# Unread matmuls of 512 columns on TensorE in the opening of an attention and expert kernel

## The chip, the cores and the metric

The kernel runs on one core of a Trainium2 chip. The metric is device time in microseconds (us), from launch to the end of the core's work. The core has TensorE (matrix products, PE in the rows; PEld is its weight load), VectorE (DVE), ScalarE (ACT), GpSimd (POOL) and SyncE (SP, which here only issues DMAs). Each engine works its own queue in order, and waits on semaphores for the others. [...]

## The reference

Attention over 4 batches, 8 heads, 768 positions, head size 64, with a linear distance bias and a window of 96 keys besides 8 global ones; then a gate that gives each of the 3072 tokens to one of 8 experts of 384 places; then the experts' two matrix products.

```python
scores = scale * np.matmul(q, k.transpose(0, 1, 3, 2))
is_global = pos[None, :] < int(n_global)
is_local = (rel >= 0) & (rel < int(n_local))
scores = scores + bias[None, :, :, :]
scores = np.where(is_global | is_local, scores, -1000000000.0)
a = np.exp(scores - np.max(scores, axis=-1, keepdims=True))
attn = np.matmul(a / np.sum(a, axis=-1, keepdims=True), v)
...
logits = x @ w_gate          # tokens are given out by falling logit, 384 to an expert
out[mask] = np.maximum(x[mask] @ w1[e], 0.0) @ w2[e]
```

## The kernel before

Attention runs in 8 **units**. Unit u holds four heads of one batch (two units to a batch), that is two pairs of heads, n = 2u ("a") and n = 2u + 1 ("b"). The keys are cut into 7 tiles of 120 keys with the 8 global keys in front of each; a tile is seen by a window of 216 queries. The tiles are in three groups: 0 and 1, 2 and 3, 4 to 6. The steps have short names, with the unit or pair that they work on:

- KT, QT: VectorE transposes keys or queries in blocks (line 278). KB (ScalarE, 286), KS (GpSimd, 292 and 293) put the keys in place for TensorE; QO (303) does so for the queries.
- S0, S1, S2: TensorE's scores of the three groups, in f32, four heads side by side in strips of 32 rows (line 335). An f32 matmul shows as two instructions in the trace. S0 has 32 instructions, S1 has 32, S2 has 48. They write the PSUM banks ps0 and ps1, of which there is one set; only S1 of unit 0 writes the four spare banks po0, po1, t0 and t1 (named psx).
- BI: VectorE adds the distance bias and takes the scores out of PSUM into P (line 353), two instructions to a pair. The next group's scores need the banks that BI has read. EX: ScalarE's exponential on P (360). M0, M1: GpSimd adds up what a sum over keys needs (369 to 376).
- AV0, AV1: TensorE's product with the values (393), two halves of the queries. OT: ScalarE copies it out (400). SU: TensorE's sums and gate products (410, 414), into t0 or t1. LT: VectorE takes these out. TK, TO: transposes of finished outputs for the token matrix (492 and 511), from unit 1 on.

The order on every engine is written by hand. Unit 0 and the first half of unit 1 stand one step after the other (lines 613 to 664 of before); after that a loop goes through the table ORDER once for every turn, and each entry has a stage: an entry with stage 3 works on the unit three turns back. So in one turn TensorE has S1 and S2 of one unit, AV and SU of the unit before, and S0 of the unit after. In turn 3 the entries that matter here are BI0b and BI0a of unit 1 (VectorE), then S1 of unit 1 (TensorE), then AV0b, SUa of unit 0, then S2 of unit 1. Turn 2 has S0 of unit 1 for TensorE, and for VectorE the transposes of unit 2.

The constant `ones_bf` (128 x 128, bf16) is filled by GpSimd at the start (line 71). The loads of keys and queries stand in SyncE's queue, ahead of all units that use them; five buffers go round. After attention come the routing (131 to 160 us in the trace), with matmuls (`fill`, line 732) whose results nobody reads, and then the experts.

Of the kernel before, what the change touches and what calls it, by code (L numbers as in the profile page):

```python
# [9 lines left out]
FP32 = mybir.dt.float32  # L10
# [32 lines left out]
def kernel(  # L43
# [12 lines left out]
    nc = tc.nc  # L56
# [13 lines left out]
    ones_bf = consts.tile([128, 128], BF16)  # L70
# [137 lines left out]
    with ExitStack() as actx:  # L208
# [4 lines left out]
        def distances():  # L213
            nc.gpsimd.iota(Dm[:, WA:WB], pattern=[[1, QW]], base=N_GLOBAL, channel_multiplier=-1,
                           allow_small_or_imprecise_dtypes=True)
            nc.gpsimd.affine_select(out=Dm[:, WA:WB], in_=Dm[:, WA:WB], compare_op=ALU.is_ge, fill=FAR,
                                    base=N_GLOBAL, pattern=[[1, QW]], channel_multiplier=-1)
            nc.gpsimd.affine_select(out=Dm[:, WA:WB], in_=Dm[:, WA:WB], compare_op=ALU.is_ge, fill=FAR,
                                    base=N_LOCAL - 1 - N_GLOBAL, pattern=[[-1, QW]], channel_multiplier=1)
            nc.gpsimd.tensor_copy(out=Dm[:, W0A:WA], in_=Dm[:, WA:WB])  # L220
            nc.gpsimd.memset(Dm[0:N_GLOBAL, WA:WB], FAR)
            nc.gpsimd.memset(Dm[0:N_GLOBAL, WA : WA + KT], float(N_LOCAL))
            nc.gpsimd.memset(Dm[0:N_GLOBAL, W0A:WA], FAR)
            nc.gpsimd.memset(Dm[0:N_GLOBAL, W0A : W0A + KT], float(N_LOCAL))
            nc.gpsimd.affine_select(out=Dm[0:N_GLOBAL, W0A : W0A + 60], in_=Dm[0:N_GLOBAL, W0A : W0A + 60],
                                    compare_op=ALU.is_ge, fill=FAR, base=-1, pattern=[[-1, 60]], channel_multiplier=1)
            nc.gpsimd.affine_select(out=Dm[0:N_GLOBAL, W0A + 60 : W0A + KT], in_=Dm[0:N_GLOBAL, W0A + 60 : W0A + KT],
                                    compare_op=ALU.is_ge, fill=FAR, base=60 - N_LOCAL, pattern=[[1, 60]],
                                    channel_multiplier=-1)
            nc.gpsimd.tensor_copy(out=Dm[:, WB:WC], in_=Dm[:, WA : WA + WC - WB])  # L230
            nc.gpsimd.tensor_copy(out=Dm[:, WC:NW], in_=Dm[:, WA : WA + NW - WC])
# [10 lines left out]
        ps_t = actx.enter_context(tc.tile_pool(name="ps_t", bufs=1, space=bass.MemoryType.PSUM))  # L242
# [13 lines left out]
        def load(kind, u):  # L256
            b, hf = divmod(u, 2)
            m = (2 * u + (kind == "q")) % NRAW
            t = w_early[:, RAW * m : RAW * (m + 1)].bitcast(FP32).rearrange("p (j d) -> p j d", d=D_)
            nc.sync.dma_start(t.rearrange("p j d -> p (j d)"),  # L260
                              (k if kind == "k" else q)[b, 4 * hf : 4 * hf + 4].rearrange("a (c j) d -> (a c) (j d)", j=NJ))
            raws[kind, u] = t
# [21 lines left out]
        def kA_big(u, g, i0=0, i1=NT - 1):  # L284
            t = tTs["k", u, g].rearrange("p j c -> p c j")
            nc.scalar.copy(out=kAs[u % 2][:, g, i0:i1, 8:128].rearrange("p i (c j) -> p i c j", j=NJ),  # L286
                           in_=t[:, i0 * NC5 : i1 * NC5, :].rearrange("p (i c) j -> p i c j", c=NC5))
# [19 lines left out]
        for p in (2, 3, 4, 5, 6, 7, 0, 1):  # L307
            m, e, hf = p // 4, p // 2 % 2, p % 2
# [7 lines left out]
        def weight_piece():  # L316
            if wpieces:
                dst, s_ = wpieces.pop(0)
                nc.gpsimd.dma_start(dst, s_)
# [204 lines left out]
        def consts_(*which):  # L524
            for i in which:
                late[i]()
# [7 lines left out]
        pss = {}  # L534
        pieces = {}
        done = set()
        WP = {4: 1, 5: 3, 6: 4}

        def step(op, u):
# [61 lines left out]
            elif k == "WT":  # L601
                for _ in range(WP.get(u + 1, 0)):
                    weight_piece()
# [3 lines left out]
        def steps(ops, u=0):  # L607
            for op in ops.split():
                step(op, u)

        stage = dict((o.split(":")[0], int(o.split(":")[1])) for o in ORDER)

        with tc.manual_schedule():
            load("k", 0)
            load("q", 0)
            distances()
            nc.sync.dma_start(wg_sb, moe_w_gate.rearrange("(kc p) e -> p kc e", p=128))
            load("k", 1)
            for i in range(2):
                nc.vector.memset(kAs[i][:, :, NT - 1, 8 + LASTK : 128], 0.0)  # L620
            for i in range(NB):
                nc.vector.memset(v7s[i][:, :, NT - 1, :], 0.0)
            load("q", 1)
            load_v(0)
            load("k", 2)
            steps("KT0 KT1")
            for g in range(2):
                kA_big(0, g, 0, 2)
                kA_small(0, g)
            steps("QT0 QT1")  # L630
            qT_out(0, 0, 0, 14)
            qT_out(0, 1, 0, 14, dve=True)
            consts_(0, 2)
            for t in range(2):
                nc.gpsimd.tensor_scalar(out=wgx[64 * t : 64 * t + 64, :, 8 * t : 8 * t + 8],  # L635
                                        in0=wg_sb[64 * t : 64 * t + 64], scalar1=LSCALE, scalar2=None, op0=ALU.mult)
            consts_(11, 12, 13)
            load_v(1)
            steps("S0")
            for g in range(2):  # L640
                kA_big(0, g, 2)
                qT_out(0, g, 14, 32, dve=True)
            for g in range(2):
                done.update([(f"KB{g}", 0), (f"KS{g}", 0), (f"QO{g}", 0)])
            steps("BI0a BI0b EX0a")
            load_v(2)
            steps("S1")
            steps("KT0 KS0", 1)
            steps("BI1a BI1b")
            consts_(14, 3)  # L650
            steps("KB0", 1)
            steps("EX1a")
            steps("KT1 KS1 QT0", 1)
            load_v(3)
            consts_(1, 6)
            steps("S2 BI2a EX2a M0a M1a")
            qT_out(1, 0, dve=True)
            done.add(("QO0", 1))
            steps("QT1", 1)
            steps("BI2b")  # L660
            steps("KB1", 1)
            qT_out(1, 1, dve=True)
            done.add(("QO1", 1))
            steps("EX0b AV0a OT0a AV1a OT1a EX1b EX2b M0b")
            consts_(5, 10, 15, 16)
            it0 = 1 + stage["S0"]
            for it in range(it0, NU + max(stage.values())):
                for o in ORDER:
                    op = o.split(":")[0]
                    step(op, it - stage[op])  # L670
            assert len(done) >= NU * len(ORDER), len(done)
            while wpieces:
                weight_piece()
# [451 lines left out]
    op = ctx.enter_context(tc.tile_pool(name="op", bufs=4))  # L1125
# [43 lines left out]
```

## Time and profile before

| | |
|---|---|
| median of 3 runs | 273.35 us (271.0, 273.35, 273.55) |
| profiled execution, its own time | 269.57 us |
| its span, first to last instruction | 267.9 us |
| mean granted clock of TensorE | 0.945 |
| PE busy | 232.1 us (87%) |
| DVE, ACT, POOL busy | 150.5, 153.5, 153.3 us (56 to 57%) |

The profiled execution is one run of its own, and every duration below comes from it. Its span plus 1.67 us is its time. In an order of time a row is a merged stretch: start, length, engine, line, what is written <- what is read, size, how many instructions, and in brackets how long the engine sat idle before it and what ended that. A stretch's length holds the tail of its last matmul, so the next one can begin before it ends; the distance of two starts is the better measure.

### The profile page before, as it was taken

The page shows a single profiled execution, that of the slowest core. Times are in us where ns is not written, and L with a number is a line of the kernel's source. Part 1 is how long each engine was busy: PE and PEld are TensorE (multiplying, and loading weights), DVE is VectorE, ACT ScalarE, POOL GpSimd, SP SyncE. Part 2 cuts the span into 40 slices and gives each one's busy share as a digit, 9 for nine tenths or more (in the row PEclk, how much of TensorE's full clock was granted, in tenths as well). Part 3 has the DMA queues.
Part 4 walks back from the last instruction along what each step waited for, and adds up shares of the span by engine and source line. Part 5 has one row for each costly group of instructions (what it writes and reads, how often), then busy time and mean ns, then how long its engine had stood idle before and what let it go on. Part 6 is the DMA issues. An engine that isn't in the chain of part 4 may idle for free. (4 is left out here: it accounts for less than half of the span.)

```text
span 267.9 us, 6769 instructions
## 1 busy us (share of the span) xinstructions
PE 232.1 (87%) x2681; PEld 164.4 (61%) x2681; DVE 150.5 (56%) x332; ACT 153.5 (57%) x304; POOL 153.3 (57%) x283
## 2 busy tenths in 40 slices
PE   0675599999998999999878888999999989999960
PEld 0654478888886888878657651956555545555520
DVE  3699678879998976564787772132321412323130
ACT  2549658999989999645678860525235051432500
POOL 6878734749585989968311004757565564741240
PEclk9997579999999999999999995899999999999995
DMA  6998976675455399990699991599999999330221
GB/s 246 339 356 214 269 291 190 151 225 125 134 111 111 56 183 206 191 216 7 97 180 220 241 299 48 109 218 244 243 267 240 268 238 303 131 138 36 84 91 37
DMA packets 49862, 49.22 MB, mean 184 GB/s; under 512 B 29344, under 2 KB 41376, under 8 KB 49824
## 3 DMA queue, kind: packets, MB, share of 16 engines
q0 software_dynamic: 15680, 26.22, 46.6%
q1 hardware_dynamic: 34144, 22.50, 30.4%
q8 instruction: 23, 0.38, 0.6%
q14 instruction: 15, 0.12, 0.1%
HBM read 56.05 MB, written 9.44 MB: 244 GB/s over the span
## 5 line engine op out<-in xcount | busy, mean ns | idle before, releaser
L1082 ACT ACTIVATE hT<-ph 128x384 bf16<-128x384 f32 (+2 forms) x72 | 32.6, 454 | 62.5 <-PE ph L1079 60.9
L335 PE MATMUL ps<-qT,kA 32*128 32x216 f32 (+2 forms) x864 | 47.9, 358 | 15.0 <-POOL wgx L635 9.3
L353 DVE SCALAR_TENSOR_TENSOR P<-Dm,ps 128x432 f32<-128x432 f32 x92 | 49.2, 595 | 13.9 <-PE ps L335 13.8
L335 PEld LDWEIGHTS ps<-qT,kA 32*128 32x128 f32 x864 | 40.6, 200 | 20.1 <-POOL wgx L635 9.3
L372 POOL TENSOR_TENSOR S<-P 128x576 f32<-128x576 f32 (+1 forms) x32 | 39.0, 1218 | 19.9 <-ACT P L360 14.8
L360 ACT ACTIVATE P<-P 128x864 f32<-128x864 f32 x48 | 42.6, 923 | 13.5 <-DVE P L353 12.7
L393 PE MATMUL po<-P,v 128*64 128x216 f32 (+6 forms) x576 | 43.3, 299 | 2.9 <-ACT P L360 2.7
L393 PEld LDWEIGHTS po<-P,v 128*64 128x64 f32 x576 | 36.0, 139 | 12.5 <-ACT P L360 3.4
L1111 POOL DMA_INDIRECT out_dram<-ot,ido x24 | 23.6, 984 | 28.5 <-DVE ot L1110 25.3
L1057 POOL DMA_INDIRECT xe<-x_tok,idi x24 | 23.3, 969 | 26.8 <-PE pw L732 18.6
L1110 DVE COPY ot<-po 128x512 f32<-128x512 f32 x24 | 16.4, 691 | 30.9 <-PE po L1107 24.4
L1107 PEld LDWEIGHTS <-hT 128*128 128x128 bf16 x192 | 18.2, 98 | 19.2
L1073 DVE COPY xT<-pxe 128x512 bf16<-128x512 bf16 x24 | 9.5, 422 | 35.8 <-PE pxe L1070 35.0
L507 ACT ACTIVATE x<-pw,ri 128x64 bf16<-128x64 f32 x112 | 24.6, 363 | 5.7 <-PE pw L492 5.4
L286 ACT COPY kA<-tT_k 128x720 f32<-128x720 f32 (+2 forms) x18 | 23.9, 1339 | 5.5 <-DVE tT_k L278 5.5
L1107 PE MATMUL po<-w_late,hT 128*128 128x512 bf16 x96 | 22.0, 379 | 0.0
L1079 PE MATMUL ph<-xT,w_late 128*128 128x384 bf16 x128 | 21.5, 326 | 0.0
L400 ACT COPY oT<-po 128x384 f32<-128x384 f32 x32 | 14.5, 477 | 11.8 <-PE po L393 11.8
L303 ACT COPY qT<-tT_q 128x768 f32<-128x768 f32 (+1 forms) x13 | 19.7, 1512 | 0.6 <-DVE tT_q L278 0.6
L278 DVE STREAM_TRANSPOSE tT_k<-w_early 128x768 f32<-128x768 f32 x16 | 15.3, 969 | 6.6 <-DMA w_early<-in_k_dram 3.5
L1079 PEld LDWEIGHTS <-w_late 128*128 128x128 bf16 x128 | 12.5, 98 | 8.7
L278 DVE STREAM_TRANSPOSE tT_q<-w_early 128x768 f32<-128x768 f32 x16 | 14.9, 944 | 0.2 <-DMA w_early<-in_q_dram 0.2
(166 smaller groups left out, 309.2 us busy)
## 6 DMA issues: line engine op xcount, KB each, us to landing
w_late<-in_moe_w_dram POOLq DMA_DIRECT2D x8, 1024.0 KB, 11.9
w_early<-in_k_dram SPq DMA_DIRECT2D x8, 768.0 KB
w_early<-in_q_dram SPq DMA_DIRECT2D x8, 768.0 KB
v<-in_v_dram SPq DMA_DIRECT2D x32, 180.0 KB
w_early<-in_moe_w_dram POOLq DMA_DIRECT2D x8, 512.0 KB, 8.9
w_last<-in_moe_w_dram POOLq DMA_DIRECT2D x4, 1024.0 KB, 12.6
x_tok<-x SPq DMA_DIRECT2D x2, 768.0 KB
x_tok<-x SPq DMA_DIRECT2D x2, 384.0 KB
```

What stands on the lines that cost most here:

```text
L278: nc.vector.transpose(out=t, in_=raws[kind, u][:, :, 32 * g : 32 * g + 32])
L286: nc.scalar.copy(out=kAs[u % 2][:, g, i0:i1, 8:128].rearrange("p i (c j) -> p i c j", j=NJ), in_=t[:, i0 * NC5 : i1 * NC5, :].rearrange("p ...
L335: nc.tensor.matmul(at(a)[:, o : o + w], lhsT=kA[r, gd, i, :], rhs=qTt[r, gd, KT * i : KT * i + w], start=(gd == 0), stop=(gd == 1), skip_g ...
L353: nc.vector.scalar_tensor_tensor(out=Ps[n][:, 2 * g : 2 * g + 2, t, :], in0=W, scalar=-8.0 * slopes[2 * (n % NPAIR) + t], in1=st[:, 0 : 2 ...
L360: nc.scalar.activation(P, P, AF.Exp, scale=0.125)
L372: nc.gpsimd.tensor_tensor(out=to[:, :, :, 0:OV], in0=P[:, i0 : i0 + m, :, 0:OV], in1=P[:, i0 - 1 : i0 + m - 1, :, KT:QW], op=ALU.add)
L393: nc.tensor.matmul(po[n, bank][64 * t : 64 * t + 64, a - QB * bank : z - QB * bank], lhsT=v7[:, t, i, :], rhs=Ps[n][:, min(i, 5), t, a - q ...
L507: nc.scalar.activation(x[:, 2 * hf + i, 128 * jj + 64 * t : 128 * jj + 64 * t + 64], ps[:, i, 64 * t : 64 * t + 64], AF.Identity, scale=ri ...
L1079: nc.tensor.matmul(ph[:, 128 * t0 : 128 * t1], lhsT=w1_of(e)[:, kc, 128 * fc : 128 * fc + 128], rhs=xT_of[e][:, kc, t0:t1, :].rearrange("p ...
L1082: nc.scalar.activation(hT[:, fc, 128 * t0 : 128 * t1], ph[:, 128 * t0 : 128 * t1], AF.Relu)
L1107: nc.tensor.matmul(po, lhsT=hT[:, fc, 128 * t : 128 * t + 128], rhs=w2_of(e)[:, fc, :], start=(fc == 0), stop=(fc == NFC - 1))
L1111: s = nc.gpsimd.indirect_dma_start(out=out[:, :], out_offset=bass.IndirectOffsetOnAxis(ap=ido[:, TSLAB * e + t : TSLAB * e + t + 1], axis= ...
```

## The change

It adds a function `warm(n)`. It takes one of the banks t0 and t1 in turn, and issues n matmuls into it as one accumulation: `ones_bf` as weights, and `ones_bf` four times over as 512 columns. Nothing reads the result. It is called four times: with 20 ahead of everything else on TensorE (bank t0), with 7 between AV0a and AV1a of unit 0 (t1), with 4 ahead of S0 of unit 1 (t0), and with 14 ahead of S1 of unit 1 (t1).

```diff
+        warms = []
+
+        def warm(n):
+            i = len(warms) % 2
+            t = ps_t.tile([128, 512], FP32, tag=f"t{i}", name=f"warm{len(warms)}")
+            warms.append(t)
+            for m in range(n):
+                nc.tensor.matmul(t, lhsT=ones_bf, rhs=ones_bf.rearrange("p (o n) -> p o n", o=1).to_broadcast([128, 4, 128]),
+                                 start=(m == 0), stop=(m == n - 1))
+
...
             load("k", 0)
             load("q", 0)
+            warm(20)
             distances()
...
-            steps("EX0b AV0a OT0a AV1a OT1a EX1b EX2b M0b")
+            steps("EX0b AV0a OT0a")
+            warm(7)
+            steps("AV1a OT1a EX1b EX2b M0b")
+            warm(4)
             consts_(5, 10, 15, 16)
...
                     op = o.split(":")[0]
+                    if (op, it - stage[op]) == ("S1", 1):
+                        warm(14)
                     step(op, it - stage[op])
```

The instructions of VectorE, ScalarE, GpSimd and SyncE stand in the same order before and after. TensorE's rows follow at three places. In brackets stand the engines whose semaphores an instruction waits for.

TensorE's queue at the start of the program, before; `ps_0_0` are the banks of S0 of unit 0:

```order
L1164 UNCONDITIONAL_BRANCH [waits barrier_Pool_Activation_PE_DVE_SP_release]
L335 MATMUL ps_0_0_215<-qT_196,kA_135 128x216 [waits Activation_49,Pool_49]
L335 MATMUL ps_0_0_215<-qT_196,kA_135 128x216
L335 MATMUL ps_0_0_216<-qT_196,kA_135 128x216 x2
L335 MATMUL ps_0_0_215<-qT_196,kA_135 128x216 [waits DVE_49,Pool_49]
```

And with the change, where `warm` is the bank of the 20:

```order
L1180 UNCONDITIONAL_BRANCH [waits barrier_Pool_Activation_PE_DVE_SP_release]
L544 LDWEIGHTS ones_bf [waits Pool_49]
L544 MATMUL warm_145<-ones_bf 128x512
...
L544 LDWEIGHTS ones_bf
L544 MATMUL warm_145<-ones_bf 128x512
L335 MATMUL ps_0_0_236<-qT_217,kA_135 128x216 [waits Activation_49,Pool_49]
L335 MATMUL ps_0_0_236<-qT_217,kA_135 128x216
L335 MATMUL ps_0_0_237<-qT_217,kA_135 128x216 x2
L335 MATMUL ps_0_0_236<-qT_217,kA_135 128x216 [waits DVE_49,Pool_49]
```

The first instruction of TensorE is now a weight load that waits for GpSimd (the fill of `ones_bf`), and 20 pairs of load and matmul stand ahead of S0. S0's own waits are the same.

TensorE from the middle of AV0a to S0 of unit 1, before; `po` are the outputs, `ps_1_0` the banks of S0 of unit 1:

```order
L393 MATMUL po_0_344<-P_237,v_0_137 64x144 [waits Activation_49]
L393 MATMUL po_0_344<-P_237,v_0_137 64x144 [waits DVE_49]
L393 MATMUL po_0_344<-P_237,v_0_137 64x24 x2
L393 MATMUL po_0_355<-P_237,v_0_137 64x72 [waits PE_49]
...
L393 MATMUL po_0_355<-P_237,v_0_137 64x192 x2
L393 MATMUL po_0_355<-P_237,v_0_137 64x216 [waits Activation_49]
...
L393 MATMUL po_0_355<-P_237,v_0_137 64x48
L335 MATMUL ps_1_0_401<-qT_334,kA_136 128x216 [waits DVE_49,PE_49,Pool_49]
...
L335 MATMUL ps_1_0_402<-qT_334,kA_136 128x216 [waits DVE_49,PE_49]
```

And with the change:

```order
L393 MATMUL po_0_365<-P_258,v_0_137 64x144 [waits Activation_49]
L393 MATMUL po_0_365<-P_258,v_0_137 64x144 [waits DVE_49]
L393 MATMUL po_0_365<-P_258,v_0_137 64x24 x2
L544 LDWEIGHTS ones_bf
L544 MATMUL warm_376<-ones_bf 128x512 [waits DVE_49]
...
L544 LDWEIGHTS ones_bf
L544 MATMUL warm_376<-ones_bf 128x512
L393 MATMUL po_0_384<-P_258,v_0_137 64x72 x2
...
L393 MATMUL po_0_384<-P_258,v_0_137 64x216 [waits Activation_49]
...
L544 LDWEIGHTS ones_bf
L544 MATMUL warm_407<-ones_bf 128x512
...
L335 MATMUL ps_1_0_435<-qT_355,kA_136 128x216 [waits DVE_49,PE_49,Pool_49]
```

The 7 stand between AV0a and AV1a. Their first matmul waits for VectorE, which has to have read the bank. The 4 stand between AV1a and S0, with no wait on another engine.

TensorE from the end of S0 to S1 of unit 1, before; `ps_1_1` are the banks of S1:

```order
L335 MATMUL ps_1_0_402<-qT_334,kA_136 128x216 x2
...
L335 MATMUL ps_1_0_401<-qT_334,kA_136 128x216 x2
L335 MATMUL ps_1_0_402<-qT_334,kA_136 128x216 x2
L335 MATMUL ps_1_1_431<-qT_334,kA_136 128x216 [waits DVE_49,PE_49]
L335 MATMUL ps_1_1_431<-qT_334,kA_136 128x216
L335 MATMUL ps_1_1_432<-qT_334,kA_136 128x216 [waits PE_49]
L335 MATMUL ps_1_1_432<-qT_334,kA_136 128x216
```

And with the change:

```order
L335 MATMUL ps_1_0_435<-qT_355,kA_136 128x216 x2
...
L335 MATMUL ps_1_0_435<-qT_355,kA_136 128x216 x2
L335 MATMUL ps_1_0_436<-qT_355,kA_136 128x216 x2
L544 LDWEIGHTS ones_bf
L544 MATMUL warm_465<-ones_bf 128x512 [waits PE_49]
...
L544 LDWEIGHTS ones_bf
L544 MATMUL warm_465<-ones_bf 128x512
L335 MATMUL ps_1_1_480<-qT_355,kA_136 128x216 [waits DVE_49,PE_49]
L335 MATMUL ps_1_1_480<-qT_355,kA_136 128x216
L335 MATMUL ps_1_1_481<-qT_355,kA_136 128x216 [waits PE_49]
```

The 14 stand behind S0. S1's first instruction, which waits for VectorE (BI0 of unit 1), is now behind them.

## Rows read from the trace of the kernel before

**Rows 1.** The page, part 1: busy time, share of the span, instructions.

```profile
PE 232.1 (87%) x2681; PEld 164.4 (61%) x2681; DVE 150.5 (56%) x332; ACT 153.5 (57%) x304; POOL 153.3 (57%) x283
```

**Rows 2.** TensorE in order of time: start, length, line, operation, [idle before <- releaser].

```profile
9.32 3.26 PE L335 MATMUL ps<-qT,kA 32*128 32x216 f32 x32 [9.32 <-POOL wgx L635]
12.33 1.93 PE L335 MATMUL psx<-qT,kA 32*128 32x216 f32 x32
...
18.13 1.03 PE L393 MATMUL po<-P,v 128*64 128x144 f32 x16 [0.32 <-ACT P L360]
21.51 0.97 PE L393 MATMUL po<-P,v 128*64 128x216 f32 x12 [2.35 <-ACT P L360]
...
24.33 3.37 PE L335 MATMUL ps<-qT,kA 32*128 32x216 f32 x28 [1.25 <-DVE P L353]
30.65 3.26 PE L335 MATMUL ps<-qT,kA 32*128 32x216 f32 x32 [2.95 <-DVE P L353]
...
37.53 0.65 PE L335 MATMUL ps<-qT,kA 32*128 32x216 f32 x8
```

**Rows 3.** Stretches: busy time (count) of five engines, granted clock, DMA share, GB/s.

```profile
9.30:12.30 3.00, 2.98 (x32) 3.00 (x36) 1.38 (x4) 1.78 (x2) 2.82 (x4) 1.00 1.20 300
...
22.80:23.20 0.40, 0.28 (x4) 0.00 (x0) 0.40 (x2) 0.40 (x2) 0.40 (x1) 0.94 0.31 68
...
24.30:27.70 3.40, 3.37 (x28) 2.52 (x28) 3.40 (x5) 3.40 (x5) 2.21 (x7) 0.50 1.03 303
...
30.65:36.80 6.15, 6.15 (x60) 4.84 (x64) 3.60 (x6) 3.83 (x4) 1.67 (x4) 0.50 1.07 321
36.80:38.00 1.20, 1.20 (x28) 0.81 (x24) 0.49 (x2) 1.20 (x2) 0.55 (x2) 1.00 0.09 21
...
60.00:128.00 68.00, 66.65 (x1202) 54.86 (x1197) 51.84 (x106) 54.83 (x68) 55.27 (x112) 1.00 0.69 133
...
160.00:170.00 10.00, 8.60 (x54) 4.43 (x52) 1.42 (x6) 1.31 (x5) 5.30 (x6) 0.50 0.26 81
```

**Rows 4.** VectorE in order of time, 12.69 to 31.4 us.

```profile
12.69 2.15 DVE L353 SCALAR_TENSOR_TENSOR P<-Dm,ps 128x432 f32<-128x432 f32 x4 [2.01 <-PE ps L335]
...
15.64 2.11 DVE L353 SCALAR_TENSOR_TENSOR P<-Dm,psx 128x432 f32<-128x432 f32 x4
...
28.38 2.12 DVE L353 SCALAR_TENSOR_TENSOR P<-Dm,ps 128x432 f32<-128x432 f32 x4
30.41 0.97 DVE L278 STREAM_TRANSPOSE tT_k<-w_early 128x768 f32<-128x768 f32 x1
```

**Rows 5.** ScalarE in order of time, two places.

```profile
8.40 0.77 ACT L303 COPY qT<-tT_q 128x336 f32<-128x336 f32 x1 [0.59 <-DVE tT_q L278]
...
40.92 0.48 ACT L400 COPY oT<-po 128x384 f32<-128x384 f32 x1 [2.06 <-PE po L393]
```

**Rows 6.** TensorE in order of time, unit 2 from S1 to S2.

```profile
46.03 1.74 PE L335 MATMUL ps<-qT,kA 32*128 32x216 f32 x32
...
50.24 0.44 PE L492 MATMUL t<-ident,oT 128*128 128x128 f32 x2
50.61 1.96 PE L335 MATMUL ps<-qT,kA 32*128 32x216 f32 x48
```

**Rows 7.** TensorE in order of time, bf16 matmuls of 512 columns.

```profile
154.55 1.68 PE L732 MATMUL pw<-w_early,ident_bf 128*128 128x512 bf16 x4
...
160.55 5.08 PE L732 MATMUL pw<-w_early,ident_bf 128*128 128x512 bf16 x8
...
175.69 4.70 PE L1107 MATMUL po<-w_early,hT 128*128 128x512 bf16 x21
```

**Rows 8.** GpSimd in order of time, the fill of ones_bf.

```profile
0.94 0.20 POOL L71 MEMSET ones_bf<- 128x128 bf16 x1
```

**Rows 9.** SyncE's DMA issues in order of time, keys of unit 3.

```profile
12.02 0.33 SPq L260 DMA_DIRECT2D w_early<-in_k_dram  x1
```

## The prediction

> **What bounds the kernel now.** I read the page first: TensorE is busy 87% of the span, no other engine above 57% [rows 1]. So I went to TensorE's order of time in the first 38 us [rows 2], then to the granted clock of stretches [rows 3], and last to what the other engines do at the waits [rows 4, 5].
>
> From 60 to 128 us TensorE is busy 66.65 of 68 us at full clock, while VectorE has 51.84 and ScalarE 54.83 [rows 3]. Attention is bound by TensorE there. So what TensorE gains before 38 us should arrive at the end, unless another engine cannot follow.
>
> Before 38 us it is different. TensorE starts at 9.32 and waits for VectorE at 24.33 (1.25 us) and at 30.65 (2.95 us), and for ScalarE at 21.51 (2.35 us) [rows 2]. From 30.65 on it has no wait up to 37.53 and beyond: S1, AV0b, SUa and S2 follow each other. The place to watch is therefore **S2 of unit 1 at 37.53**: by how much it comes earlier is what the change is worth.
>
> Two clocks run here. S0 of unit 0 takes 3.26 us for 32 instructions [rows 2], S1 of unit 2 takes 1.74 for 32 of the same form [rows 6]. The first is the price of half clock: S1 of unit 1, at a granted clock of 0.50, also takes 3.26 [rows 2, 3]. The clock column reads 1.00 at 9.3 to 12.3, but the durations say half, and I go by them: nothing was recorded before the first rise. By 12.33 the clock is up, after 3.0 us of work. It falls near 23.2, after two gaps (0.32 and 2.35) and little work, and it rises again at 36.8, after 6.15 us of unbroken work from 30.65 [rows 2, 3]. [...]
>
> **The change, part by part.** It adds 45 matmuls of 512 columns, each with its weight load, to TensorE's queue and moves nothing on another engine.
>
> *Price of one.* In a group on one bank at full clock, 21 take 4.70 us: 0.224 each. At half clock the trace has such matmuls only with a wait after each (every one has the bank to itself): eight in 5.08 us, 0.63 each, at 160.55, where the clock reads 0.50, against four in 1.68, 0.42 each, at full clock [rows 3, 7]. The difference, 0.21, is the clock's; so 0.43 each in a group at half clock (an estimate from these rows).
>
> *Group of 20.* It waits for GpSimd's fill of ones_bf, over at 1.14 [rows 8]; I take 1.2 as its start. Its cover is TensorE's idle time up to 9.32 [rows 2]. The clock rises after 3.0 to 6.2 us of work (the two rises above). After 3.0 us, 7 are done and 13 x 0.224 = 2.9 remain: end at 7.1. After 6.2 us, 14 are done and 6 remain: end at 8.7. Both lie before 9.32, so S0 is not delayed, and it starts 0.6 to 2.2 us after a busy stretch. If no rise came at all, 20 x 0.43 = 8.6 would end at 9.8 and delay S0 by 0.5.
>
> *What S0 at full clock gives.* 3.26 - 1.74 = **1.52 us**. S0 starts when ScalarE's query copy of 8.40 ends at 9.17 [rows 5], as before. VectorE is done with its query copies at 10.68 and sits idle 2.01 until 12.69, waiting for S0 [rows 4]; it would start its bias at 11.17. From 12.69 to 31.4 VectorE has no idle time at all: 14 rows in a chain, biases, transposes and copies of units 0 to 3 [rows 4]. The whole chain moves by 1.52 if its inputs are there. No row of the chain waits for a load, and the loads have room: the last of them, the keys of unit 3, is issued at 12.02 [rows 9] and used at 30.41. So the bias of unit 1 that releases S1, 28.38 to 30.50 [rows 4], ends at 28.98. Bounds: 0 (S0 stays at half clock) to 1.52; I take 1.52.
>
> *Groups of 7 and 4.* The 7 stand behind AV0a and ahead of AV1a, whose second half waits 2.35 us for ScalarE at 21.51 [rows 2]. 7 x 0.224 = 1.6 fits into that wait. The wait on VectorE that the first of them carries is for the bias of S1's second pair, which VectorE ends by 17.75 [rows 4], before AV0a's second half starts at 18.13. The 4 (0.9 us) stand ahead of S0 of unit 1, which waits 1.25 us behind its first four instructions [rows 2]; they fit as well. At half clock they cost 3.0 and 1.7 and overrun by about 1 us in all; but S0 of unit 1 has slack, ending at 27.70 before and used at 28.38. Cost: 0. Behind them in the queue stand AV1a and S0 of unit 1 only.
>
> *Group of 14.* It stands between S0 and S1 of unit 1, where TensorE is idle 2.95 us. S0 of unit 1 can start at 24.33 - 1.52 = 22.8, waits some 0.7 for the last query copy, and ends about 24.8 at full clock. 14 x 0.224 = 3.1 brings TensorE to 27.9, still 1.1 us before S1's release at 28.98. Cost: 0. That cover is gone where one costs more than 4.2/14 = 0.30 us, that is at half clock.
>
> *What S1 to S2 at full clock gives.* S1 to S2 of unit 1 take 37.53 - 30.65 = 6.88 us. The same stretch of the next unit, all at full clock, takes 50.61 - 46.03 = 4.58, of which 0.37 is a pair of transposes (50.24) that unit 1 does not have [rows 6]: 4.21. The gain is **2.67 us**. VectorE has to deliver S2's banks in time: S1 from about 29.1 ends at 30.9, four biases of 2.15 in all (as at 12.69 [rows 4]) end at 33.1, and S2 would start at 29.1 + 4.2 = 33.3. It holds, with 0.2 us left. Bounds: 0 to 2.67; I take 2.67.
>
> *After 37.53.* ScalarE waits 2.06 us for TensorE at 40.92 [rows 5], so it is pulled forward and not behind. No other stage has work tied to a fixed moment.
>
> **Sum.** 1.52 + 2.67 = 4.2 us. Against the profiled execution, 269.57 - 4.2 = 265.4. The runs shown lie above it: 271.0, 273.35 and 273.55. The lifts over the profiled execution are 0, 1.4, 3.8 and 4.0; the median of the four is 2.6. The forecast is 265.4 + 2.6 = **268.0 us**, 2.0% below the median shown. Where these lifts come from no row here tells. One candidate: the clock is also at 0.50 from 160 to 170 us, between the routing and the experts [rows 3], and in another execution it may fall elsewhere. The change does nothing for that.
>
> **Rivals.**
> *The clock still falls in the middle.* The groups do not fill every gap: about 0.7 us ahead of AV0a's second half, 0.9 ahead of AV1a's, and 1.1 ahead of S1 stay open by my times. Against it: the fall of before came after 2.35 us without work, and no gap left is that long. Then the second term is lost and the first kept: 269.57 - 1.5 = 268.0 by the profile, **270.7** with the lift. Chance 0.17.
> *Only the second term holds.* S0 starts at half clock again after up to 2.2 us of idle, or is held by its inputs. Gain 2.67: 266.9, **269.5** with the lift. Chance 0.08.
> *The lead is given back.* Part of the half-clock time was not on the path after all, because VectorE, with 0.2 us left at S2, or ScalarE cannot follow. For it: ScalarE is 81% and VectorE 76% busy from 60 to 128 [rows 3], so a lost lead is not caught up. Against it: both wait for TensorE around 38 us. A gain of 1.5 to 2.5 would remain: about 267.6, **270.2** with the lift. Chance 0.10.
> [...]
> *Slower.* The groups run at half clock and get in the way. The place is the group of 14. S0 of unit 0 late by 0.5, S0 of unit 1 ends at 28.2, 14 x 0.43 = 6.0, and S1 starts at 34.2 instead of 30.65. If the clock stays low up to S2, that comes at 41.1, 3.5 us late: 273.1 by the profile, **275.7** with the lift. It decides from 0.30 us for one matmul of that group on. Against it: this would be some 10 us of unbroken work, and both rises of before came within 6.2. If the clock does rise in it, S2 is late by 0.9 only. Chance 0.05.
>
> **How the numbers follow.** Forecast 0.60, the others 0.17, 0.08, 0.10 and 0.05. A measurement of this kernel can tell about 1% (2.7 us) from no change. The forecast and the second rival lie at 4.2 and 2.67; given the spread of 2.6 us in the runs shown I count 0.56 of 0.60 and half of 0.08 as faster, and a third of the rival with the lead given back: 0.64 faster. Same: 0.30. Slower: the last rival and a little spread, 0.06. The range: from the sum with no lift and a little more, 264.8, to the first rival with the highest lift (268.0 + 4.0), 272.0. That leaves out the slower case and the ends of the spread.
>
> **What would show it.** In the profile after: the 20 end before 9.3 and change pace on the way from about 0.43 to 0.22 us; S0 of unit 0 takes about 1.75 us; VectorE's first bias starts near 11.2; the granted clock reads 1.00 from there through 38 us; the 14 end before S1's bank is released, near 29.0; S1 to S2 takes 4.2 us, with S2 near 33.3; and from there to the last matmul all is as before but 4.2 us earlier. The prediction is wrong where a stretch at 0.50 appears between 12 and 37 us, where S1 starts right behind the last unread matmul, or where TensorE shows new waits from VectorE or ScalarE between 33 and 128 us.

## The result, and the profile after

| | before | changed |
|---|---|---|
| median of 4 runs | 272.33 us (271.0 to 273.55) | 268.95 us (268.47 to 269.42) |
| ratio | | 0.9884, 95% interval [0.9846, 0.9922] |
| profiled execution | 269.57 us, span 267.9 | 268.92 us, span 267.2 |

The change makes the kernel 1.2% faster, by 0.8 to 1.5%. The time was foretold as 268.0 us. But the two profiled executions differ by 0.65 us only, and where the rest lies has to be found first.

TensorE in order of time with the change (start, length, line, operation, [idle before <- releaser]); it answers to [rows 2]:

```profile
1.20 7.05 PE L544 MATMUL warm<-ones_bf 128*128 128x512 bf16 x20 [1.20 <-POOL ones_bf L71]
9.27 1.92 PE L335 MATMUL ps<-qT,kA 32*128 32x216 f32 x32 [1.02 <-ACT qT L303]
10.98 1.67 PE L335 MATMUL psx<-qT,kA 32*128 32x216 f32 x32
...
17.21 1.68 PE L544 MATMUL warm<-ones_bf 128*128 128x512 bf16 x7
...
20.13 0.97 PE L393 MATMUL po<-P,v 128*64 128x216 f32 x12 [0.63 <-ACT P L360]
21.03 1.04 PE L544 MATMUL warm<-ones_bf 128*128 128x512 bf16 x4
...
22.98 0.64 PE L335 MATMUL ps<-qT,kA 32*128 32x216 f32 x4 [0.34 <-DVE P L353]
...
25.12 3.19 PE L544 MATMUL warm<-ones_bf 128*128 128x512 bf16 x14
29.31 1.74 PE L335 MATMUL ps<-qT,kA 32*128 32x216 f32 x32 [0.99 <-DVE P L353]
...
33.30 2.02 PE L335 MATMUL ps<-qT,kA 32*128 32x216 f32 x48
```

The 20 end at 8.25. S0 of unit 0 takes 1.71 us to the start of S1 (9.27 to 10.98), where it took 3.01. The 7 and the 4 stand in waits of which 0.63 and 0.34 us are left. The 14 end at 28.3, S1 of unit 1 waits another 0.99 us for VectorE and starts at 29.31. S2 of unit 1 starts at 33.30, against 37.53: 4.2 us earlier.

VectorE in order of time; it answers to [rows 4]:

```profile
11.30 2.15 DVE L353 SCALAR_TENSOR_TENSOR P<-Dm,ps 128x432 f32<-128x432 f32 x4 [0.65 <-PE ps L335]
...
27.06 2.11 DVE L353 SCALAR_TENSOR_TENSOR P<-Dm,ps 128x432 f32<-128x432 f32 x4
...
31.08 2.15 DVE L353 SCALAR_TENSOR_TENSOR P<-Dm,ps 128x432 f32<-128x432 f32 x4 [1.03 <-PE ps L335]
```

The first bias starts at 11.30 and not at 12.69, and the chain behind it, again without a gap, brings S1's release 1.3 us forward.

Stretches (busy time and count of five engines, granted clock, DMA share, GB/s); they answer to [rows 3]:

```profile
9.00:12.00 3.00, 2.73 (x56) 2.56 (x60) 2.35 (x7) 2.06 (x3) 2.76 (x5) 1.00 1.09 312
...
27.00:30.00 3.00, 2.01 (x23) 1.11 (x24) 3.00 (x6) 1.25 (x2) 2.79 (x15) 1.00 1.12 293
30.00:33.00 3.00, 3.00 (x60) 2.41 (x56) 1.97 (x5) 2.33 (x3) 0.94 (x3) 1.00 1.14 225
...
60.00:128.00 68.00, 66.10 (x1169) 54.39 (x1163) 51.15 (x111) 53.23 (x76) 52.56 (x105) 1.00 0.69 130
```

The clock reads 1.00 in all of them, and TensorE is busy 66.10 of 68 us from 60 to 128, as before (66.65). The routing's first matmul comes at 124.76 here, at 129.04 before: the lead is still 4.3 us. It is lost in the first expert. TensorE again, from the routing on:

```profile
124.76 0.87 PE L492 MATMUL pw<-ident,oT 128*128 128x128 f32 x6 [0.51 <-DVE LT L432]
...
166.42 0.82 PE L1086 MATMUL pxe<-ident_bf,xe 128*128 128x128 bf16 x8
...
169.87 0.38 PE L1086 MATMUL pxe<-ident_bf,xe 128*128 128x128 bf16 x4 [2.41 <-DVE xT L1089]
...
170.34 5.29 PE L1095 MATMUL ph<-xT,w_early 128*128 128x256 bf16 x32
...
180.44 5.36 PE L1095 MATMUL ph<-xT,w_early 128*128 128x384 bf16 x32
```

The third row waits 2.41 us for VectorE's copy of a transposed slab. Behind this wait the clock falls to half from 170.3 to 173.7 us, and the fourth row, with 256 columns, runs in it. The stretch from 171 to 172:

```profile
171.00:172.00 1.00, 1.00 (x6) 0.73 (x5) 0.41 (x1) 0.34 (x1) 0.76 (x1) 0.50 1.09 207
```

Expert 1 (the first stretch with 384 columns) starts at 180.44, where it started at 180.22 before. From the routing's first matmul to that stretch, called **the routing distance** below, it is 55.7 us here and 51.2 before. That the time is 1.2% better all the same asks for more traces of both kernels.

### The profile page after: what moved, and what is told of

Same layout as the page of the kernel before. It is cut to its first block, busy times and chain, and to the rows that moved or that the text cites. A ratio compares the mean times of both kernels' runs of the same rounds, so it can differ in the third digit from the quotient of the medians.

```text
span 267.2 us, 6850 instructions
## 1 busy us (share of the span) xinstructions
PE 241.1 (90%) x2717; PEld 165.9 (62%) x2726; DVE 150.3 (56%) x332; ACT 153.8 (58%) x304; POOL 153.2 (57%) x283
## 5 line engine op out<-in xcount | busy, mean ns | idle before, releaser
L353 DVE SCALAR_TENSOR_TENSOR P<-Dm,ps 128x432 f32<-128x432 f32 x92 | 49.1, 593 | 10.9 <-PE ps L335 10.8
L335 PE MATMUL ps<-qT,kA 32*128 32x216 f32 (+2 forms) x864 | 44.0, 334 | 4.0 <-DVE P L353 2.8
L393 PE MATMUL po<-P,v 128*64 128x216 f32 (+6 forms) x576 | 42.5, 294 | 1.1 <-ACT P L360 0.9
L335 PEld LDWEIGHTS ps<-qT,kA 32*128 32x128 f32 x864 | 37.1, 185 | 10.2 <-issue 5.2
L393 PEld LDWEIGHTS po<-P,v 128*64 128x64 f32 x576 | 35.4, 137 | 10.5 <-issue 2.3
L1123 PE MATMUL po<-w_late,hT 128*128 128x512 bf16 x92 | 21.2, 379 | 0.0
L400 ACT COPY oT<-po 128x384 f32<-128x384 f32 x32 | 14.6, 480 | 10.2 <-PE po L393 10.2
```

The source lines that it names most:

```text
L335: nc.tensor.matmul(at(a)[:, o : o + w], lhsT=kA[r, gd, i, :], rhs=qTt[r, gd, KT * i : KT * i + w], start=(gd == 0), stop=(gd == 1), skip_g ...
L353: nc.vector.scalar_tensor_tensor(out=Ps[n][:, 2 * g : 2 * g + 2, t, :], in0=W, scalar=-8.0 * slopes[2 * (n % NPAIR) + t], in1=st[:, 0 : 2 ...
L393: nc.tensor.matmul(po[n, bank][64 * t : 64 * t + 64, a - QB * bank : z - QB * bank], lhsT=v7[:, t, i, :], rhs=Ps[n][:, min(i, 5), t, a - q ...
L1123: nc.tensor.matmul(po, lhsT=hT[:, fc, 128 * t : 128 * t + 128], rhs=w2_of(e)[:, fc, :], start=(fc == 0), stop=(fc == NFC - 1))
```

## The experiments

Runs of one batch share one chip and the runs of the kernel before on it. There were four batches.

**Both kernels again, and each half of the change alone.** e1 is the kernel before and e2 the changed kernel, unchanged. e3 and e4:

```diff
 # e3: the first group alone
-            warm(7)
...
-            warm(4)
...
-                    if (op, it - stage[op]) == ("S1", 1):
-                        warm(14)
 # e4: the middle groups alone
-            warm(20)
```

> The kernel before once more, for a second trace of it. In the first pair of traces the changed kernel was 4.3 us ahead at the start of the routing (124.76 against 129.04) and 0.2 us behind at the first 384-column stretch of the experts (180.44 against 180.22): the distance from the routing's first matmul to that stretch was 51.2 us before and 55.7 after. Theory A: this distance changes from execution to execution in either kernel, and the first trace of before was a short one; then it comes out anywhere between 51 and 56 here, and S2 of unit 1 starts at 36 to 37.5. Theory B: the pause in the first expert comes from the change; then it is 51.2 again, with no wait over 1 us in front of the experts' transposes.

> The changed kernel once more, for a second trace. Both theories: S2 of unit 1 at 33.3, the routing's first matmul at 124.8. Theory A: the distance from there to the first 384-column stretch is anywhere between 51 and 56. Theory B: 55.7 again, with a wait of about 2.4 us ahead of the experts' transposes, and a stretch at half clock behind it.

> The group of 20 alone. By the sum of the prediction: S0 of unit 0 takes 1.75 us, VectorE's first bias starts at 11.2 to 11.3, S1 of unit 1 starts at 29.1, and as the clock has fallen in the gaps before it, S1 to S2 takes up to 6.9 us and S2 starts at 34.5 to 36.0. Gain 1.5 us at the routing's start, 2.7 at most. If the first term were not on the path, S1 would start at 30.6. Theory B expects a long distance (55.7) here only if it comes from the start of the kernel; theory A expects any.

> The groups of 7, 4 and 14 without the 20. By the sum of the prediction: S0 of unit 0 takes 3.3 us as before, S1 of unit 1 starts at 30.6, but at full clock, and S1 to S2 takes 4.2 us: S2 at 34.8, a gain of 2.7 us at the routing's start. If the middle groups need the first one to hold the clock, S1 to S2 takes up to 6.9 and S2 comes at 37.5 or later.

Before takes 268.74 us on this chip (25 runs).

| kernel | time, us | ratio to before | S1, S2 of unit 1 | routing's first matmul | routing distance |
|---|---|---|---|---|---|
| e1, before | 269.16 | 1.0007 [0.998, 1.0034] | 30.76, 36.41 | 127.90 | 52.3 |
| e2, changed | 265.69 | 0.9896 [0.9854, 0.9937] | 29.62, 33.61 | 125.16 | 52.2 |
| e3, the 20 alone | 267.86 | 0.9967 [0.9944, 0.999] | 29.24, 35.06 | 127.58 | 51.6 |
| e4, the 7, 4 and 14 alone | 267.24 | 0.9942 [0.9922, 0.9962] | 30.48, 34.48 | 126.08 | 51.2 |

The kernel before once more, TensorE in order of time:

```profile
30.76 3.26 PE L335 MATMUL ps<-qT,kA 32*128 32x216 f32 x32 [2.95 <-DVE P L353]
...
36.41 1.96 PE L335 MATMUL ps<-qT,kA 32*128 32x216 f32 x48
...
127.90 0.87 PE L492 MATMUL pw<-ident,oT 128*128 128x128 f32 x6 [0.51 <-DVE LT L432]
...
180.22 5.37 PE L1079 MATMUL ph<-xT,w_early 128*128 128x384 bf16 x32
```

S2 comes at 36.41 and not at 37.53, since here the clock rose at 34.3 us and not at 36.8. So what the change can gain behind S1 differs from one execution of before to the next. The routing distance is 52.3 in one kernel and 52.2 in the other: theory B is out for this chip, and the changed kernel's long distance is not in the groups.

The group of 20 alone gives S1 of unit 1 at 29.24 and then 5.82 us to S2, with S1 at half clock:

```profile
29.24 3.26 PE L335 MATMUL ps<-qT,kA 32*128 32x216 f32 x32 [2.96 <-DVE P L353]
...
35.06 1.96 PE L335 MATMUL ps<-qT,kA 32*128 32x216 f32 x48
...
117.33 1.42 PE L393 MATMUL po<-P,v 128*64 128x72 f32 x20 [1.05 <-issue]
```

The middle groups alone give S1 at 30.48, as late as before, and then 4.00 us:

```profile
30.48 1.74 PE L335 MATMUL ps<-qT,kA 32*128 32x216 f32 x32 [0.99 <-DVE P L353]
...
34.48 2.02 PE L335 MATMUL ps<-qT,kA 32*128 32x216 f32 x48
```

These are the two terms of the sum, one in each kernel: about 1.3 us ahead of S1, and the stretch behind it. In times they are 0.9 and 1.5 us, and 3.05 us for the whole change; within the intervals the two add up to it. Both times are short of what their traces show at S2. e3's trace is 1.35 us ahead of e1's at S2, but only 0.3 us at the routing's start, where 1.5 was expected: it gives back 1.05 us at 117.33, in a wait for which the profile names no releaser, and no other trace has it there. e4's trace is 1.8 us ahead of e1's at the routing's start, where 2.7 was expected (1.9 at S2, as the clock of e1 had risen early), and waits 1.48 us for a gather of tokens at 217.65, where e1's waits 0.45.

One thing in e2 had been foretold only as a risk: the clock fell again behind the 20, at 10.8 us, while S0 ran. Stretches of e2:

```profile
9.30:10.80 1.50, 1.49 (x28) 1.29 (x32) 1.38 (x4) 1.50 (x2) 1.38 (x2) 1.00 1.00 358
10.80:14.20 3.40, 3.40 (x45) 3.40 (x41) 2.55 (x5) 1.20 (x2) 3.14 (x6) 0.50 1.17 284
14.20:30.00 15.80, 13.54 (x153) 8.07 (x150) 15.80 (x23) 11.13 (x12) 13.75 (x41) 1.00 0.98 290
```

The 20 ended at 7.04 in this execution, TensorE was idle 2.27 us up to 9.31, and from 10.8 to 14.2 us the clock was at half. S0 was nearly done by then, S1 of unit 0 took the loss (2.88 us to the start of S2 instead of 1.59), and S1 of unit 1 came only 0.3 us later than in the first trace. VectorE has its own work while S1 of unit 0 runs (2.55 us busy of the 3.40 at half clock).

**One group taken out of the middle, one doubled, and the routing's unread matmuls.** All from the changed kernel:

```diff
 # e5: without the 7 and the 4
-            warm(7)
...
-            warm(4)
 # e6: without the 14
-                    if (op, it - stage[op]) == ("S1", 1):
-                        warm(14)
 # e7: 28 for 14
-                        warm(14)
+                        warm(28)
 # e8: the routing's fills in groups on one bank
-            for _ in range(n):
-                pw = ps_d.tile([128, 512], FP32, tag="pk", name="pw")
-                nc.tensor.matmul(pw, lhsT=ident_bf, rhs=w1_early[:, 0, 0, 0:512], start=True, stop=True)
+            pw = ps_d.tile([128, 512], FP32, tag="pk", name="pw")
+            for m in range(n):
+                nc.tensor.matmul(pw, lhsT=ident_bf, rhs=w1_early[:, 0, 0, 0:512], start=(m == 0), stop=(m == n - 1))
...
-            fill(4)
+            fill(9)
...
-            fill(2)
+            fill(3)
...
-            fill(8)
+            fill(19)
```

> The groups of 20 and 14, without those of 7 and 4. With the group of 20 alone the clock fell at 19.5 us, so it should fall there again. Theory A (each group holds the clock across its own wait): S0 of unit 1 runs at half clock and ends near 26.2; the 14 begin at half clock, 0.43 us each, some 6 us if no rise comes, and S1 of unit 1 starts at 30.5 to 32.2, 1 to 3 us later than 29.3; S1 to S2 then takes 4.2 to 4.6 us, as the 14 have brought the clock up, and S2 starts at 35 to 36.5. Theory B (the 7 and 4 do nothing that the 14 do not do): S1 at 29.3 to 29.6 and S2 at 33.3 to 33.6, as with all four groups.

> The groups of 20, 7 and 4, without the 14. TensorE is then idle from about 25.1 to 29.3 us ahead of S1 of unit 1. Theory A (each group holds the clock across its own wait): the clock falls in that wait, S1 starts at 29.3 and takes 3.3 us, and S2 starts between 34.5 and 36.2. Theory B (the 14 are not needed): no stretch at half clock before 150 us, S2 at 33.3 to 33.6.

> 28 unread matmuls ahead of S1 of unit 1 instead of 14: 14 more at 0.224 us are 3.1 us, and 1.0 us of waiting stood behind the 14. If the wait of S1 on VectorE is what the group hides in, and TensorE sets the end from there on: S1 starts 2.1 us later, at 31.5, S2 at 35.5, and the time is 2.1 us above that of the changed kernel (0.8%). If TensorE is not what sets the end behind S1, the time stays within 0.5 us of the changed kernel's.

> The changed kernel, and in the routing's last part the unread matmuls of 512 columns put into groups on one bank, 9, 3 and 19 of them in place of 4, 2 and 8 that each wait for the one before. All traces so far are at half clock for 10 to 14 us from 154 to 160 us on, through the first expert's first slab (32 matmuls of 128 columns in 3.1 to 3.65 us). If that half clock costs time on the path: no fall there, the first slab in 2 to 2.7 us, the distance from the routing's first matmul to the first 384-column stretch about 50.3 instead of 51.2 to 52.3, and 0.5 to 1.5 us less than the changed kernel. If the gathers set the pace there, the clock stays up and the distance does not change; if the groups are too long, the first expert's transposes start later and the time rises.

This chip gives the kernel before 272.69 us (23 runs), near the 272.33 of the result.

| kernel | time, us | ratio to before | S1, S2 of unit 1 | routing's first matmul | routing distance |
|---|---|---|---|---|---|
| e5, without 7 and 4 | 270.01 | 0.9903 [0.9862, 0.9943] | 30.82, 34.81 | 126.37 | 54.5 |
| e6, without 14 | 270.57 | 0.993 [0.9898, 0.9963] | 29.21, 35.79 | 127.21 | 54.5 |
| e7, 28 for 14 | 271.27 | 0.9954 [0.9922, 0.9986] | 31.20, 35.19 | 126.64 | 54.5 |
| e8, dense fills | 268.97 | 0.9883 [0.9835, 0.993] | 29.18, 33.17 | 124.75 | 55.5 |

TensorE in e5, around S1 of unit 1:

```profile
22.91 3.36 PE L335 MATMUL ps<-qT,kA 32*128 32x216 f32 x28 [1.25 <-DVE P L353]
26.20 4.69 PE L544 MATMUL warm<-ones_bf 128*128 128x512 bf16 x14
30.82 1.74 PE L335 MATMUL ps<-qT,kA 32*128 32x216 f32 x32
```

S0 of unit 1 runs at half clock (granted 0.50 from 22.4 to 29.2 us; 3.36 us for 28 instructions), the 14 take 4.69 us and not 3.19, S1 starts behind them without a wait, and S1 to S2 is 3.99. Theory A, but that S1 to S2 took less than the expected 4.2 to 4.6, so that S2 came 0.2 us before the expected 35. TensorE in e6:

```profile
29.21 3.26 PE L335 MATMUL ps<-qT,kA 32*128 32x216 f32 x32 [4.12 <-DVE P L353]
...
35.79 1.96 PE L335 MATMUL ps<-qT,kA 32*128 32x216 f32 x48
```

S1 is in time, and takes 3.26 us behind a wait of 4.12 us, at a granted clock of 0.50 from 29.2 to 34.7. So the 14 hold the clock across their wait, and so do the 7 and 4, which were only taken out together; no other group did it for them. e8, which leaves the opening as in the changed kernel, stands for that kernel on this chip. By the traces, the 7 and 4 are worth 1.6 us and the 14 are worth 2.6 here (S2 at 34.81 and 35.79 against 33.17 in e8); the ratios of e5 and of the changed kernel cannot be told apart.

TensorE in e7:

```profile
25.05 6.22 PE L544 MATMUL warm<-ones_bf 128*128 128x512 bf16 x28
31.20 1.74 PE L335 MATMUL ps<-qT,kA 32*128 32x216 f32 x32
```

28 unread matmuls take 6.22 us. S1 starts 2.0 us later than with 14, and so do S2 and the routing (2.0 and 1.9 us later than in e8 on the same chip). By the ratios to before the time is 0.7% above e8's and the changed kernel's, some 1.9 us, and 2.3 us above e8's by the medians, where 2.1 was expected; the intervals of e7 and e8 overlap a little. What TensorE loses at S1 reaches the routing in full. That it reaches the end in full is what the times suggest, but these two traces do not show it: their spans differ by 0.8 us only, as e8 loses 1.0 us more behind the routing (below). The cover of the 14 was the wait on VectorE and no more.

Stretches of e8, from the end of the routing:

```profile
156.00:163.00 7.00, 5.07 (x34) 2.44 (x33) 1.43 (x6) 0.00 (x0) 3.04 (x4) 1.00 0.18 58
163.00:166.40 3.40, 3.06 (x28) 2.90 (x28) 0.00 (x0) 1.35 (x5) 2.79 (x3) 0.50 0.41 116
```

In the other traces the clock falls between 153.8 and 159.7; here it holds until 163.0. The ratio is that of the changed kernel: no gain that these runs can tell. But the first expert's first slab still runs at half clock, so what it would give to hold the clock through it was not reached.

The routing distance of 55.5 is near the 55.7 of the changed kernel's first trace, and 1.0 us longer than the 54.5 of e5, e6 and e7 on this chip. These two traces have what the other three lack: behind the wait in the first expert (2.11 us here) the clock falls a second time, here from 169.8 to 173.3, and the row with 256 columns runs in it:

```profile
170.37 5.06 PE L1095 MATMUL ph<-xT,w_early 128*128 128x256 bf16 x32
```

It takes 5.06 us here and 5.29 in the first trace, against 3.66 at full clock in e10 (below).

**Both kernels once more, and another order on VectorE.** e9 is the kernel before, e10 the changed kernel. e11, from the changed kernel:

```diff
+            defer = {("QT0", 2): ("BI0a", 1), ("QT1", 2): ("BI1b", 1), ("KT0", 3): ("LTa", 0),
+                     ("KT1", 3): ("BI2b", 1), ("QT0", 3): ("BI2b", 1)}
...
-                    if (op, it - stage[op]) == ("S1", 1):
-                        warm(14)
-                    step(op, it - stage[op])
+                    u = it - stage[op]
+                    if (op, u) in defer:
+                        continue
+                    if (op, u) == ("S1", 1):
+                        warm(10)
+                    step(op, u)
+                    for k_ in [k_ for k_ in defer if defer[k_] == (op, u)]:
+                        del defer[k_]
+                        step(*k_)
```

> The kernel before a third time, beside the next two on one chip. In the traces so far the distance from the routing's first matmul to the first 384-column stretch was 51.2 to 52.3 us in one batch, where before takes 268.7 us, and 54.5 to 55.5 in the other, where before takes 272.7. Theory C: the distance belongs to the chip and not to the kernel; so here 51 to 52.5 if before takes about 269, and 54 to 56 if it takes about 272.5. Theory D: the long distance belongs to kernels with the groups; then it is 51.2 to 52.3 here whatever the time of before is.

> The changed kernel a third time, on the chip of the other two. Theory C: the same distance as the kernel before has on this chip, within 1 us. Theory D: 54 to 56. Both: S2 of unit 1 at 33.2 to 33.6, and a time 1.0 to 1.2% below the kernel before.

> The changed kernel with another order on VectorE around S1 of unit 1. In the trace of the changed kernel S0 of unit 1 ends at 25.1 us, but its biases, which release S1, start at 27.06 only, behind four transposes of unit 2. Here the two query transposes of unit 2 stand behind the biases (one behind BI0a, one behind BI1b), three transposes of unit 3 go behind LTa and BI2b, and the group of 14 has 10. Theory E (VectorE's chain is what S1 waits for, and TensorE sets the end from there): biases at 25.3, S1 at 27.5, S2 at 31.6, 1.7 us less than the changed kernel. Theory F (VectorE has no slack to pay it back): S2 of unit 1 is early, but a later stretch of scores waits for VectorE by about as much, and S0 of unit 3 and the time are within 0.5 us of the changed kernel's.

| kernel | time, us | ratio to before | S1, S2 of unit 1 | routing's first matmul | routing distance |
|---|---|---|---|---|---|
| e9, before | 268.94 | 0.9996 [0.9975, 1.0018] | 30.49, 36.76 | 128.27 | 52.6 |
| e10, changed | 265.58 | 0.9871 [0.9833, 0.9909] | 29.38, 33.38 | 124.88 | 52.2 |
| e11, transposes behind | 265.61 | 0.986 [0.9813, 0.9906] | 27.70, 31.69 | 125.27 | 51.1 |

Before takes 268.92 us on this chip. The routing distance is the same in both kernels again, as theory C has it. The changed kernel from the routing on, TensorE, beside the rows of the first trace above:

```profile
124.88 0.88 PE L492 MATMUL pw<-ident,oT 128*128 128x128 f32 x6 [0.51 <-DVE LT L432]
...
167.07 0.79 PE L1086 MATMUL pxe<-ident_bf,xe 128*128 128x128 bf16 x8
...
168.16 0.38 PE L1086 MATMUL pxe<-ident_bf,xe 128*128 128x128 bf16 x4
...
168.59 3.66 PE L1095 MATMUL ph<-xT,w_early 128*128 128x256 bf16 x32
...
177.06 5.36 PE L1095 MATMUL ph<-xT,w_early 128*128 128x384 bf16 x32
```

There is no wait ahead of the third row here. What stood there in the first trace is seen on ScalarE. Its copies of the first expert's hidden layer, in the first trace:

```profile
167.93 0.28 ACT L1098 ACTIVATE hT<-ph 128x128 bf16<-128x128 f32 x1 [0.47 <-PE pxe L1086]
168.67 0.28 ACT L1098 ACTIVATE hT<-ph 128x128 bf16<-128x128 f32 x1 [0.47 <-PE pxe L1086]
```

and in e10, the whole stretch in one piece:

```profile
164.37 3.22 ACT L1098 ACTIVATE hT<-ph 128x128 bf16<-128x128 f32 x8 [9.77 <-PE ph L1095]
```

In the first trace the last ones come 0.74 us apart, with 0.47 us of waiting for TensorE before each, though TensorE's own rows were done by 167.5. What holds them up there is not shown by these profiles.

e11 brings S1 of unit 1 to 27.70, as theory E has it, and S2 to 31.69. But the lead is gone by the routing. VectorE in order of time:

```profile
25.42 2.13 DVE L353 SCALAR_TENSOR_TENSOR P<-Dm,ps 128x432 f32<-128x432 f32 x4
...
33.81 2.11 DVE L353 SCALAR_TENSOR_TENSOR P<-Dm,ps 128x432 f32<-128x432 f32 x4
...
38.95 2.11 DVE L353 SCALAR_TENSOR_TENSOR P<-Dm,ps 128x432 f32<-128x432 f32 x4
```

and TensorE:

```profile
27.70 1.74 PE L335 MATMUL ps<-qT,kA 32*128 32x216 f32 x32
...
31.69 2.01 PE L335 MATMUL ps<-qT,kA 32*128 32x216 f32 x48
...
41.20 1.74 PE L335 MATMUL ps<-qT,kA 32*128 32x216 f32 x32 [0.91 <-DVE P L353]
...
49.98 0.20 PE L393 MATMUL po<-P,v 128*64 128x48 f32 x1 [1.11 <-issue]
```

VectorE now runs without a gap from 29.5 to 41.9 (the biases of S2 at 33.81, those of S0 of unit 2 at 38.95), and S1 of unit 2 waits 0.91 us for it at 41.20. S2 of unit 2 then starts at 45.56, against 46.54 in e10: of the lead of 1.7 us VectorE has taken 0.7, as theory F has it, and 1.0 is left. That goes at 49.98, in a wait of 1.11 us with no releaser in the profile, like the one of e3 at 117.33. Whether it belongs to the order or to this execution stays open: the profiled execution took 268.28 us, the longest of the four (the others 264.62, 264.87 and 266.35), and it also waits 2.10 us for a gather at 217.03, where e10 waits 0.33. The medians are the same as the changed kernel's, with too few runs to tell 1 us. No kernel tried beats the changed one by what these runs can tell.

**The kernel before a fourth time.**

> The kernel before a fourth time, for a trace on a chip where it takes about 272.5 us, if this is one. Where the chip gives that time: theory C (the long distance from the routing's first matmul to the first 384-column stretch belongs to the chip) expects 54 to 56 us here, with a wait of 1 us or more in the first expert; theory D (it belongs to kernels with the groups) expects 51.2 to 52.6. Where the chip gives about 269 us, both expect 51.2 to 52.6, and the question stays open.

This chip gave before 269.49 us (e12 itself 268.97, ratio 0.9985 [0.9964, 1.0007]), and the routing distance was 52.6, with S1 at 30.51 and S2 at 36.76. So a trace of the kernel before from a chip of the 272.5 us kind is still missing. Each batch ran on another chip, and none came twice, so that the chip makes the difference, and not the hour, is likely but not shown.

## Why the prediction was right, and where its sum was off

The time fell in the range, and on the right side, by the mechanism that was forecast. The number alone would not show that: the range reached up to 272.0, just under the median of before, and 268.95 lies nearer to the second rival's 269.5 than to 268.0. The traces and e3 and e4 show it, with both terms on the path. Step by step:

- **The price and the cover of the groups.** 14 matmuls took 3.19 us, 0.228 each (0.224 forecast). The 20 ended at 8.25 in the first trace, 7.04 in e2 and 8.54 in e10 (7.1 to 8.7 forecast). They changed pace on the way: in the first trace a single one lasts 0.63 us up to 6 us and 0.38 from 7 us on, each with its tail. The cover held: e7 shows what it costs when it does not.
- **The first term, 1.52 us.** S0's row became 1.34 us shorter (3.26 to 1.92) and not 1.52. At S1 of unit 1 the gain is 1.2 us: 30.60 in the mean of the four traces of before (30.65, 30.76, 30.49, 30.51) against 29.44 of the changed kernel (29.31, 29.62, 29.38). VectorE's first bias came at 11.30 and not at 11.17; in e2 the half clock behind S0 took 0.3 more, and in e10 S0 started 0.2 us later than in e9 (9.36 and 9.16).
- **The second term, 2.67 us.** This is the step that was mis-sized most. S1 to S2 with the change takes 3.99 to 4.00 us in all three traces, even below the 4.21 taken. But before it takes 6.88, 5.65, 6.27 and 6.25 us, because the clock rose at 36.8, 34.3, 35.3 and 35.2 us. The trace that the prediction had was the slowest of the four. The mean is 6.26, and the term 2.3 us. It had been taken from one execution with bounds of 0 and 2.67 for what the groups might fail to do; that the price in the kernel before itself varies was left out.
- **The lead carries.** From S2 of unit 1 to the routing's first matmul it is 91.5 us in all four traces of before and 91.5 to 91.6 in all three of the changed kernel, whatever the start. The rival in which VectorE or ScalarE gives the lead back did not happen at this lead. With 1.7 us more, in e11, VectorE gave 0.7 of it back; where the rest went stays open.
- **The sum.** With the terms as measured it is 1.2 + 2.3 = 3.4 us. The medians differ by 3.4 (272.33 to 268.95), 3.05 (e2) and 3.3 us (e10). The forecast was 0.95 us too low: 0.8 by this sum, forecast at 4.2, and the rest by the lift.
- **The lift.** The prediction could not say why the runs of before lie up to 4.0 us above its profiled execution. The runs show that before takes 267.6 to 270.4 us on three chips and 271.0 to 274.9 on the others. The profiled execution, 269.57, lies in the first band, and the runs of the result in the second. So the first pair of traces most likely comes from two kinds of chip, and the 0.65 us between them is not what the change does. The difference between the kinds shows in the routing distance, 51.1 to 52.6 against 54.5 to 55.7; of the slow kind only kernels with groups were traced, but before takes 3.5 us more there, as the changed kernel does (268.95 against 265.6). The lift of 2.6, taken from the spread of the runs, was right in size (the median of before lies 2.8 us above its profiled execution), but by luck, as the prediction had no cause for it. Its one candidate, half clock between the routing and the experts, does not show as one: that stretch lasts 10.2 us in the profiled execution of 269.57 us, and 13.6 to 13.7 in the three other traces of before, which took 268.9 to 269.0.
- **The rival on the clock's fall.** No trace of the changed kernel has half clock between 14.2 and 150 us. One has it from 10.8 to 14.2 (e2), the place that the prediction had named as a risk, though there it cost 0.3 us and not the whole first term.

By the medians the gain is 3.05 to 3.4 us, by the ratios 1.0 to 1.3%, and each ratio's interval reaches below 1%. On the path of the traces the two stretches, between which the clock falls a second time, cost 3.4 us, 1.3% of the span.

## What to carry to other kernels

In this kernel unread matmuls paid (3.05 to 3.4 us by the medians) where TensorE waits early for another engine and has a dense stretch of its own behind the wait: S1 to S2 of unit 1 took 3.99 to 4.00 us with them and 5.65 to 6.88 in the kernel before. For another kernel, price such a stretch at both clocks from rows of the same trace, and size each group to end ahead of the wait's release: in e7, 14 matmuls more (3.03 us) at a wait with 0.99 us left brought S1 and S2 2.0 us later than in e8. Whatever the other groups did, the stretch behind a group that was left out ran at half clock: S0 of unit 0 without the 20 (e4, 3.26 us), S0 of unit 1 without the 7 and 4 (e5, 3.36 us for 28 instructions), S1 of unit 1 without the 14 (e6, 3.26 us). A term that rests on when the clock rises (36.8, 34.3, 35.3 and 35.2 us in the four traces of before) should be taken from several executions of the kernel before, and two profiles are only compared after their times have been held against runs on the same chip.

## What had not been expected of the hardware

- The same program takes 268.7 to 269.5 us in three batches and 272.3 to 272.7 in the runs of the result and the second batch (e5 to e8), 1.3% apart. In the kernels with groups most of it sits in one place, the first expert behind the routing; for the kernel before this is not shown.
- Holding the clock up to 163.0 us (e8), and not to 153.8 to 159.7, gave nothing that can be measured (ratio 0.9883, and 0.9884 for the changed kernel). Half clock in the first expert does have a price: in two traces the clock fell a second time there, behind waits of 2.41 and 2.11 us, and the row with 256 columns took 5.29 and 5.06 us and not 3.66.
- The clock column reads 1.00 from the start of the changed kernel too, although the first of the 20 last 0.63 us there and the last 0.38. The durations tell there, and not the column.
